# One crossbar DMA for the x of a tile, a later place for the second part of w_in, and a planner that dates the first weights later

## The chip, the cores and the metric

The kernel runs on one NeuronCore of a Trainium2 chip. The metric is the time of one execution on the device, in microseconds (us). Four executions of the kernel before gave 237.15, 240.17, 237.21 and 239.96 us, a median of 238.58 us. One further execution was recorded by the hardware profiler: it took 237.9 us, and the span between its first and its last instruction is 236.1 us.

The engines are called PE (TensorE, matrix products; its weight loads are listed apart as PEld), ACT (ScalarE), DVE (VectorE), POOL (GpSimd) and SP (SyncE, which issues most DMAs here). A DMA is issued by an engine's queue and moves its data by itself.

## What is computed

An attention in which some heads see all earlier positions and the others only a few first positions ("sinks") and a window, and behind it a dense layer with an unusual activation. The reference, cut to what matters:

```python
# q, k, v: [4 batches, 8 heads, 768 positions, 64]; n_sink 4, window 64
scores = q @ k.T / 8                     # per head
keep = causal if retrieval[head] else causal & (is_sink | in_window)
a = softmax(where(keep, scores, -1e9))
x = (a @ v) laid out as [3072 tokens, 512]
h = x @ w_in                             # [512, 2048]
g = h - tanh(h)
out = g @ w_out                          # [2048, 512], float32
```

## The kernel before, in words

**Tiling.** The 3072 tokens are cut into 12 tiles of 256 tokens (TT = 256), three to a batch (NG = 3), each of two blocks of 128 (NB = 2). Heads go in pairs: HP = 4 pairs, 128 columns each. For each tile and pair the kernel computes scores (`st_S`, matmul L971), their exponential on ACT (L991), masks on DVE, a product with v (`st_A`, matmul L1060, tile `av`), and the division by the row sum on DVE. What results is x of the tile, 256 tokens by 512 columns, in float16. The dense layer needs it transposed, as `xT`. With it `H_unit(t, u)` makes 256 of the 2048 hidden columns of tile t in 16 matmuls (L1165, tile `ph`, two accumulations of 4 column blocks each for two groups of 128 columns), tanh on ACT (L1178, `th`), and h - tanh(h) on DVE (L1185, `gt`). There are 8 units to a tile. `O_group` multiplies by w_out (L1224, tile `po`), ACT copies the result out (L1200) and SP stores it (L1212).

**How x is transposed.** Tiles 0 to 2 (the first batch) do it on PE: `st_X` transposes a pair's two blocks (L1138, tile `xp`) and ACT or DVE copies them from PSUM into `xT` (L853, L855). Tiles 3 to 11 are "ranked" (`ranked(t)`: heads sorted so that those that see everything come first). Their x is collected in one tile `x16t` of [128, 2 blocks, 8 heads, 64] by DVE (L1090), and `st_X_tile` turns it with crossbar DMAs that SP issues (L1118): one for each block of 128 tokens, 512 columns each, into `xT` of shape [128, 4, 256]. Each has its own key, and the matmuls of `H_unit` wait for both (`x_keys`). Crossbar DMAs of 1024 columns are in the kernel too: `cast_ranked` turns q and k of a block together (L727), two such DMAs for each ranked tile.

**Weights.** POOL issues the DMAs that load and cast weights: w_in in four parts of 512 columns (`load_w_in`, L415; the table `W_IN`), w_out in four parts (`load_w_out`, L429). Part j of w_in feeds units 2j and 2j+1 of a tile. The same POOL queue carries v of tile 1, q, k and v of tile 2 (`load_cast`, L392). All of these are chained by `behind`: each may be issued only after the one before it has been issued. So the order on the queue is: w_in part 1, v of tile 1 (two DMAs), w_in parts 2, 3 and 4, w_out part 1, q and k of tile 2 (four), w_out part 2, v of tile 2 (two), w_out parts 3 and 4.

POOL has other work in the same microseconds: it casts q and k of tile 1 from float32 to float16 (L675; four casts: q and k of the first heads, then q and k of the second heads), and it scales v by the heads' flags (L839, tile `vf`, two for tile 0).

**What sets the order.** No engine's order is written out. Each step is recorded by `op(engine, ns, fn, r, w, dma=...)` with a duration in ns, the keys that it reads and writes, and for a DMA its number of packets. `Plan.run` then plays the whole program through: each engine takes, of its steps that are ready, the one recorded first, and two DMA rings (POOL's and SP's) share the DMA time. The order that comes out is the order in which the instructions are issued; the engines keep to it on the chip whatever really comes late. L152 is where the planner says when a DMA starts to move data after its issue: 1200 ns for POOL's, 1000 or 400 ns for SP's.

```python
rings["POOL" if e == "POOL" else "SP"].append(
    [i, t + ns + (1200 if e == "POOL" else 1000 if t < 6000 else 400), each, packets * each / 16]
```

The second half of the file holds a second program, for the case that too many heads see everything; it isn't run with these inputs.

Of the kernel before, what the change touches and what calls it, by code (L numbers as in the profile page):

```python
# [8 lines left out]
FP16 = mybir.dt.float16  # L9
# [7 lines left out]
class Plan:  # L17
# [42 lines left out]
    def run(self, fill=None, until=None):  # L60
        self.fill = fill
        n = len(self.ops)
        users = [[] for _ in range(n)]
        followers = [[] for _ in range(n)]
        left = [0] * n
        for i, o in enumerate(self.ops):
            left[i] = len(o[3]) + (o[7] is not None)
            for d in o[3]:
                users[d].append(i)
            if o[7] is not None:  # L70
                followers[o[7]].append(i)
        ready = [0.0] * n
        free = dict.fromkeys(self.ENGINES, 800.0)
        queue = {e: [] for e in self.ENGINES}
        rings = {"SP": [], "POOL": []}
        now = 0.0
        self.start = [0.0] * n
        self.done = [0.0] * n
        order = []

        self.port = 0.0

        def at(i):

            return max(ready[i], self.port) if self.ops[i][6] else ready[i]

        def enqueue(i):
            queue[self.ops[i][0]].append(i)

        def finish(i, done):  # L90
            self.done[i] = done
            e, ns = self.ops[i][:2]
            for u in users[i]:
                to = self.ops[u][0]
                if to == e and e == "PE":
                    at = self.start[i] + ns
                else:
                    at = done + (60 if to == "PE" else 40)
                ready[u] = max(ready[u], at)
                left[u] -= 1  # L100
                if not left[u]:
                    enqueue(u)

        for i in range(n):
            if not left[i]:
                enqueue(i)
        while len(order) < n:
            t, e = min(
                [(max(free[e], min(at(i) for i in q)), e) for e, q in queue.items() if q],
                default=(1e12, None),  # L110
            )

            live = [r for r in rings.values() if r and r[0][1] <= now]
            nxt = min([r[0][1] for r in rings.values() if r and r[0][1] > now], default=1e12)
            if live:
                pk = sum(r[0][2] for r in live)
                end, r = min((now + r[0][3] * pk / r[0][2], k) for k, r in enumerate(live))
                stop = min(end, nxt, t)
                for x in live:
                    x[0][3] -= (stop - now) * x[0][2] / pk  # L120
                now = stop
                if end <= min(nxt, t):
                    i = live[r].pop(0)[0]
                    finish(i, now + 1300)
                    continue
                if nxt < t:
                    continue
            elif nxt < t:
                now = nxt
                continue  # L130
            now = max(now, t)
            i = min(
                (i for i in queue[e] if at(i) <= t), key=lambda i: self.ops[i][5]
            )
            queue[e].remove(i)
            _, ns, _, _, dma, _, port, _ = self.ops[i]
            if e == "PE" and t < 5600:
                ns *= 2
            self.start[i] = t
            order.append(i)  # L140
            free[e] = t + max(ns - self.OVERLAP[e], 40)
            if port:
                self.port = free[e]
            for u in followers[i]:
                ready[u] = max(ready[u], free[e])
                left[u] -= 1
                if not left[u]:
                    enqueue(u)
            if dma:
                packets, each = dma  # L150
                rings["POOL" if e == "POOL" else "SP"].append(
                    [i, t + ns + (1200 if e == "POOL" else 1000 if t < 6000 else 400), each, packets * each / 16]  # L152
                )
            else:
                finish(i, t + ns + self.RESULT[e])
        self.end = max(self.done)
        free = self.FROM
        for i in order:
            if self.ops[i][0] == "PE":
                idle = self.start[i] - free  # L160
                if self.fill and idle > 200 and i != until and self.FROM < free:
                    self.fill(int(idle * 0.5 / 107), 256)
                free = max(free, self.start[i] + self.ops[i][1])
                if i == until:
                    self.fill = None
            self.ops[i][2]()
# [3 lines left out]
def kernel(  # L170
# [98 lines left out]
    def program(first):  # L269
# [581 lines left out]
        def copy(e, dst, src):  # L851
            if e == "ACT":
                nc.scalar.copy(out=dst, in_=src)  # L853
            else:
                nc.vector.tensor_copy(out=dst, in_=src)  # L855
# [255 lines left out]

        def st_X_tile(t):

            xTs[t] = lazy(xt_pool, [128, HP, TT], FP16, "xT", f"xT{t}")
            for i in range(NB):
                op(
                    "SP", 1250,
                    lambda i=i: nc.sync.dma_start_transpose(  # L1118
                        out=xTs[t]()[:, :, i * 128 : i * 128 + 128],
                        in_=x16s[t]()[:, i, :, :].rearrange("p h d -> p (h d)"),  # L1120
                    ),
                    r=[("x16t", t)], w=[("xT", t, "all", i)], dma=(512, 22.0),
                )

        def x_keys(t):
            if ranked(t):
                return [("xT", t, "all", i) for i in range(NB)]
            return [("xT", t, c) for c in range(HP)]

        def st_X(n, tag="m", eng="DVE"):  # L1130
            t, hp = divmod(n, HP)
            if hp == 0:
                xTs[t] = lazy(xt_pool, [128, HP, TT], FP16, "xT", f"xT{t}")
            xp, key = bank([128, NB, 128], FP16, tag, f"xp{n}")

            def mm():
                for i in range(NB):
                    nc.tensor.transpose(  # L1138
                        out=xp()[:, i, :], in_=x16s[-1 - n]()[:, i, :, :], identity=ident16[:]
                    )  # L1140

            first_x.append(op("PE", 112, mm, r=[("x16", n), "ident"], w=[key]))
            op(
                eng, {"ACT": 373, "DVE": 290}[eng],
                lambda: copy(eng, xTs[t]()[:, hp, :], xp()[:].rearrange("p i c -> p (i c)")),
                r=[key], w=[("xT", t, hp)],
            )

# [6 lines left out]
        def H_unit(t, u):  # L1155
            if u == 0:
                gts[t] = lazy(g_pool, [128, NFB, TT], FP16, "gt", f"gt{t}")
            ph, key = bank([128, FU, TT], FP32, "h", f"ph{t}_{u}")
            for j in range(FU):

                def mm(j=j):
                    fb = u * FU + j
                    w, c0 = w_in_t[fb // 4]
                    for cb in range(HP):
                        nc.tensor.matmul(  # L1165
                            out=ph()[:, j, :], lhsT=w()[:, cb, c0 + fb % 4 : c0 + 512 : 4],
                            rhs=xTs[t]()[:, cb, :], start=(cb == 0), stop=(cb == HP - 1),
                        )

                op(  # L1170
                    "PE", 4 * 109, mm,
                    r=[("win", u * FU // 4)] + x_keys(t), w=[key],
                )
            th = lazy(th_pool, [128, FU, TT], FP32, "th", f"th{t}_{u}")
            tk = ("th", t * NFU + u)
            op(
                "ACT", 597,
                lambda: nc.scalar.activation(  # L1178
                    out=th()[:], in_=ph()[:], func=AF.Tanh, scale=1.0 / XS
                ),  # L1180
                r=[key], w=[tk],
            )
            op(
                "DVE", 687,
                lambda: nc.vector.scalar_tensor_tensor(  # L1185
                    out=gts[t]()[:, u * FU : (u + 1) * FU, :], in0=th()[:], scalar=-XS,
                    in1=ph()[:], op0=ALU.mult, op1=ALU.add,
                ),
                r=[key, tk], w=[("gt", t, u)],
            )  # L1190
# [131 lines left out]
            st_A(n, 1)  # L1322
            st_X(n, "o", "ACT")
        if first:
            load_w_in(*W_IN[1], ())
            load_w_in(*W_IN[2], ())
            scale_v(0, "POOL")
            load_w_in(*W_IN[3], ())
# [149 lines left out]
```

The softmax here doesn't subtract the row's maximum and nothing guards it: scores larger than these inputs give would overflow.

## Time and profile before, and how to read them

| | |
|---|---|
| four executions | 237.15, 240.17, 237.21, 239.96 us; median 238.58 us |
| the profiled execution | 237.9 us, span 236.1 us, granted PE clock 0.996 |
| PE | 223.6 us busy (95%) |
| ACT, DVE, POOL | 143.3 us (61%), 138.9 us (59%), 90.0 us (38%) |
| matmuls of x with w_in, L1165 | 768, 273 ns each |
| matmuls with w_out, L1224 | 400, 371 ns each |
| crossbar DMAs of xT, L1118 | 18, median 3.1 us from issue to landing |
| crossbar DMAs of q and k, L727 | 18, median 3.9 us |
| DMAs of w_in, L415 | 4, 512 KB each, 8.8 to 11.3 us from issue to landing |
| DMAs of w_out, L429 | 4, 512 KB each, 9.9 to 12.9 us |

All moments are microseconds from the start of the span. A line of the timeline gives the start, the duration, the engine, the line of the kernel, the operation, output and input, and how many such instructions follow each other; in brackets stands how long the engine was idle before it and what ended that. "SPq" is the issue of a DMA, not its transfer. The duration of a matmul includes its latency: successive matmuls overlap, so the start of the next says how long one really occupies PE. The view by windows gives the busy time of each engine in stretches of the span.

### The profile page before, as it was taken

To read this page: it belongs to the slowest core of one execution; us is meant where nothing else is said; L and a number is where in the kernel's file an instruction comes from. 1 tells how busy PE (TensorE), PEld (TensorE's weight loads), DVE (VectorE), ACT (ScalarE), POOL (GpSimd) and SP (SyncE) were. 2 spreads that over 40 slices of the span, in tenths; PEclk is the share of its full clock that TensorE was granted. 3 is DMA by queue.
4 is the path that set the end of the run, shared out by engine and by line. 5 is a ranking of instruction groups with operands and counts; after the bars stand their busy time and mean duration, and the time that the engine had idled before them with its cause. 6 is when DMAs were issued, how large, how long until landed. Compare 5 with 4: busy or idle time off the path is not lost. (4 is left out here: it accounts for less than half of the span.)

```text
span 236.1 us, 5930 instructions
## 1 busy us (share of the span) xinstructions
PE 223.6 (95%) x2234; PEld 158.3 (67%) x2234; DVE 138.9 (59%) x343; ACT 143.3 (61%) x221; POOL 90.0 (38%) x218
## 2 busy tenths in 40 slices
PE   7869899999999999999999999999999999999990
PEld 2446687766775787677767767767677677777660
DVE  3657667852688468658675647567676555434300
ACT  3877749883676498547668458456856754444410
POOL 5798350197709086470632929254000000000000
PEclk9999999999999999999999999999999999999998
DMA  5999999999899999988978996999303101411030
GB/s 129 265 198 207 193 186 219 215 229 219 114 219 190 227 231 173 231 186 178 202 165 221 162 237 72 242 217 151 86 0 89 45 2 47 90 44 45 2 113 29
DMA packets 106083, 35.83 MB, mean 152 GB/s; under 512 B 96194, under 2 KB 102594, under 8 KB 106050
## 3 DMA queue, kind: packets, MB, share of 16 engines
q1 hardware_dynamic: 94754, 30.03, 63.0%
q0 software_dynamic: 11008, 5.24, 16.8%
q8 instruction: 18, 0.29, 0.5%
q10 hardware_dynamic: 288, 0.14, 0.2%
q14 instruction: 15, 0.12, 0.2%
HBM read 27.27 MB, written 6.29 MB: 142 GB/s over the span
## 5 line engine op out<-in xcount | busy, mean ns | idle before, releaser
L1165 PE MATMUL ph<-xT,win 128*128 128x256 f16 x768 | 100.7, 273 | 1.8 <-DMA win<-in_moe_w_in_dram 1.0
L1224 PE MATMUL po<-wout,gt 128*128 128x512 f16 (+1 forms) x400 | 97.4, 371 | 0.3 <-ACT ot L1200 0.3
L1185 DVE SCALAR_TENSOR_TENSOR gt<-th,ph 128x512 f16<-128x512 f32 x96 | 65.4, 685 | 50.4 <-ACT th L1178 50.0
L1178 ACT ACTIVATE th<-ph 128x512 f32<-128x512 f32 x96 | 57.6, 601 | 60.8 <-PE ph L1165 56.4
L1165 PEld LDWEIGHTS <-win 128*128 128x128 f16 x768 | 80.6, 114 | 14.6 <-issue 2.2
L991 ACT ACTIVATE pt<-sc 128x1024 f16<-128x1024 f32 (+1 forms) x78 | 68.6, 927 | 8.8 <-PE sc L971 8.5
L1224 PEld LDWEIGHTS <-gt 128*128 128x128 f16 x400 | 36.4, 98 | 25.5 <-issue 1.0
L709 POOL CAST t<-raw_rqk 128x256 f16 x72 | 29.2, 443 | 56.5 <-DMA raw_rqk<-in_k_dram 41.3
L1060 PEld LDWEIGHTS <-pt 128*128 128x128 f16 x552 | 25.0, 97 | 9.7 <-DVE pt L1021 0.7
L1060 PE MATMUL av<-v,pt 128*128 128x65 f16 x304 | 25.5, 193 | 0.2 <-DVE pt L1021 0.2
L704 POOL CAST v<-raw_rv 128x128 f16 x72 | 21.6, 331 | 3.8 <-DMA raw_rv<-in_v_dram 3.8
L971 PE MATMUL sc<-qk 64*128 64x128 f16 (+1 forms) x412 | 23.1, 236 | 0.0
L1090 DVE TENSOR_TENSOR x16t<-av,rinv 128x128 f32 x72 | 20.8, 289 | 2.0 <-DMA xT<-x16t 0.2
L1200 ACT ACTIVATE ot<-po 128x512 f32<-128x512 f32 (+1 forms) x24 | 14.2, 593 | 10.7 <-PE po L1224 10.6
L971 PEld LDWEIGHTS <-qk 64*128 64x128 f16 x412 | 13.6, 94 | 9.7 <-issue 6.9
L1060 PE MATMUL av<-vf,pt 128*128 128x65 f16 x248 | 19.6, 193 | 0.0
L1016 DVE TENSOR_TENSOR pt<-pt,mS 128x512 f16<-128x512 f16 x24 | 10.9, 493 | 7.7 <-ACT pt L991 7.7
L1080 DVE RECIPROCAL rinv<-av 128x4 f32<-128x4 f32 x48 | 8.5, 178 | 11.2 <-PE av L1060 11.1
L1026 DVE TENSOR_TENSOR pt<-pt,m 128x1024 f16<-128x1024 f16 x16 | 11.9, 742 | 4.4 <-ACT pt L991 4.4
L780 POOL TENSOR_TENSOR vf<-v,rflagr 128x260 f16<-128x260 f16 x12 | 7.6, 640 | 0.0
L872 PEld LDWEIGHTS <-t 128*128 128x128 f16 x48 | 3.2, 97 | 5.8 <-ACT t L673 2.3
L459 PE MATMUL warm<-ones 128*128 128x512 f16 (+1 forms) x14 | 5.2, 527 | 1.2 <-POOL ones L454 1.2
(98 smaller groups left out, 95.0 us busy)
## 6 DMA issues: line engine op xcount, KB each, us to landing
out_dram<-ot SPq DMA_DIRECT2D x23, 256.0 KB, 2.4
raw_rqk<-in_q_dram SPq DMA_DIRECT2D x22, 256.0 KB, 4.9
raw_rqk<-in_k_dram SPq DMA_DIRECT2D x22, 256.0 KB, 4.8
raw_rv<-in_v_dram SPq DMA_DIRECT2D x18, 256.0 KB, 4.9
win<-in_moe_w_in_dram POOLq DMA_DIRECT2D x4, 512.0 KB, 9.8
wout<-in_moe_w_out_dram POOLq DMA_DIRECT2D x4, 512.0 KB, 11.7
raw_rv<-in_v_dram SPq DMA_DIRECT2D x4, 128.0 KB, 4.7
v<-in_v_dram POOLq DMA_DIRECT2D x4, 128.0 KB, 9.6
```

What stands on the lines that cost most here:

```text
L704: nc.gpsimd.tensor_copy(out=v1s[b]()[:, lo : lo + NB, rank : rank + 1, 0:D], in_=raw_of("v", t)[:, :, at, :],)
L709: nc.gpsimd.tensor_copy(out=t16[t % 2][:, :, :, rank : rank + 1, :], in_=raws["rqk", t][0]()[:, :, :, at, :],)
L971: nc.tensor.matmul(out=sc()[:, hh, o : o + nb * 128].rearrange("p (i c) -> p i c", c=128), lhsT=ks.rearrange("p i c -> p (i c)")[p_, jb * ...
L991: lambda pt=pt, gi=gi, wid=wid, sc=sc: nc.scalar.activation(out=pt()[:, :, 512 * gi : 512 * gi + wid], in_=sc()[:, :, 0:wid], func=AF.Exp, ...
L1026: nc.vector.tensor_mul(out=pv, in0=pv, in1=m4[:, h0 : h0 + 2, 256:512].unsqueeze(2).to_broadcast([128, 2, 2, 256]),)
L1060: nc.tensor.matmul(out=av()[:, i, hh, :], lhsT=pt()[:, hh, co : co + 128], rhs=vv, start=(jb == first_jb), stop=(jb == qb),)
L1090: nc.vector.tensor_mul(out=x16s[t]()[:, :, at, :], in0=av()[:, :, hh : hh + 1, 0:D], in1=rinv()[:, :, hh : hh + 1].unsqueeze(3).to_broadca ...
L1165: nc.tensor.matmul(out=ph()[:, j, :], lhsT=w()[:, cb, c0 + fb % 4 : c0 + 512 : 4], rhs=xTs[t]()[:, cb, :], start=(cb == 0), stop=(cb == HP ...
L1178: lambda: nc.scalar.activation(out=th()[:], in_=ph()[:], func=AF.Tanh, scale=1.0 / XS),
L1185: lambda: nc.vector.scalar_tensor_tensor(out=gts[t]()[:, u * FU : (u + 1) * FU, :], in0=th()[:], scalar=-XS, in1=ph()[:], op0=ALU.mult, op ...
L1200: nc.scalar.activation(out=ot()[:, c0:c1], in_=po()[:, c0:c1], func=AF.Copy, scale=1.0 / XS)
L1224: nc.tensor.matmul(out=po()[:, c0:c1], lhsT=gts[t]()[:, f, ts * 128 : ts * 128 + 128], rhs=w_out_t[f // 4]()[:, f % 4, c0:c1], start=(f == ...
```

## The change

Three edits, and what the planner makes of them.

```diff
@@ Plan.run: when POOL's DMA starts to move
-    [i, t + ns + (1200 if e == "POOL" else 1000 if t < 6000 else 400), each, packets * each / 16]
+    [i, t + ns + (1900 if e == "POOL" and t < 12000 else 1200 if e == "POOL" else 1000 if t < 6000 else 400), each, packets * each / 16]
@@ st_X_tile
-    xTs[t] = lazy(xt_pool, [128, HP, TT], FP16, "xT", f"xT{t}")
-    for i in range(NB):
-        op(
-            "SP", 1250,
-            lambda i=i: nc.sync.dma_start_transpose(
-                out=xTs[t]()[:, :, i * 128 : i * 128 + 128],
-                in_=x16s[t]()[:, i, :, :].rearrange("p h d -> p (h d)"),
-            ),
-            r=[("x16t", t)], w=[("xT", t, "all", i)], dma=(512, 22.0),
-        )
+    xTs[t] = lazy(xt_pool, [128, NB, HP, 128], FP16, "xT", f"xT{t}")
+    op(
+        "SP", 1250,
+        lambda: nc.sync.dma_start_transpose(
+            out=xTs[t]()[:].rearrange("p i c k -> p (i c) k"),
+            in_=x16s[t]()[:].rearrange("p i h d -> p (i h d)"),
+        ),
+        r=[("x16t", t)], w=[("xT", t, "all")], dma=(1024, 22.0),
+    )
@@ x_keys
-                return [("xT", t, "all", i) for i in range(NB)]
+                return [("xT", t, "all")]
@@ st_X
-                lambda: copy(eng, xTs[t]()[:, hp, :], xp()[:].rearrange("p i c -> p (i c)")),
+                lambda: copy(eng, xTs[t]()[:, :, hp, :], xp()[:]),
@@ H_unit
-                            out=ph()[:, j, :], lhsT=w()[:, cb, c0 + fb % 4 : c0 + 512 : 4],
-                            rhs=xTs[t]()[:, cb, :], start=(cb == 0), stop=(cb == HP - 1),
+                            out=ph()[:, j, :].rearrange("p (i k) -> p i k", i=NB),
+                            lhsT=w()[:, cb, c0 + fb % 4 : c0 + 512 : 4],
+                            rhs=xTs[t]()[:, :, cb, :], start=(cb == 0), stop=(cb == HP - 1),
@@ program, after tile 0
-            load_w_in(*W_IN[1], ())
+            load_w_in(*W_IN[1], t16_keys("k", 1, 0))
```

- **xT.** The tile's two blocks go in one crossbar DMA of 1024 columns instead of two of 512. `xT` is now laid out by block first, [128, 2, 4, 128], so the moving operand of the 768 matmuls of `H_unit` is two runs of 128 columns, 512 columns apart, instead of one run of 256. The copies of tiles 0 to 2 write the same two runs.
- **w_in part 2** is given a key to wait for: the float16 k of the first heads of tile 1, which POOL's second cast of tile 1 writes. Parts 3 and 4 and everything else of that chain come behind it.
- **The planner** dates the start of POOL's DMAs that are issued before 12 us by 1900 ns after their issue instead of 1200.

The order that comes out is another one on every engine. On POOL, from the first cast of tile 1 on (q0, k0, q1, k1 are its four casts):

```
before: q0, w_in 2, w_in 3, k0, scale v, scale v, q1, w_in 4, w_out 1, k1, q of tile 2 ...
after:  q0, scale v, k0, scale v, q1, w_in 2, w_in 3, w_in 4, k1, w_out 1, q of tile 2 ...
```

On PE the mask matmuls of a tile-1 unit (L958, two of 512 columns) now stand ahead of the first unit of `H_unit` instead of behind one and a half units. Around the first product with w_out the order was: two `po` steps, the second halves of attention, unit 6, unit 7 (its first half), transposes of tile 2, the transposes of x of tile 1's last pair, the other half of unit 7, tile 1's unit 0. It is now: one `po` step, half of unit 6, attention, the other half, the whole of unit 7, the transposes, the second `po` step, tile 1's unit 0. On SP the two xT issues of tile 3 followed the store of an output block directly; the single one now comes behind the load of one k block of tile 5 as well.

More of the change, by code (lines that the diff above doesn't have):

```diff
@@ L1132, in st_X @@
             if hp == 0:
-                xTs[t] = lazy(xt_pool, [128, HP, TT], FP16, "xT", f"xT{t}")
+                xTs[t] = lazy(xt_pool, [128, NB, HP, 128], FP16, "xT", f"xT{t}")
             xp, key = bank([128, NB, 128], FP16, tag, f"xp{n}")
```

## The prediction

> **What bounds the kernel now.** I read the time slices of the page first, then the windows of 6 us for how much of each PE is busy, then the timeline at the places where it isn't.
>
> ```profile
> span 236.1 us, 5930 instructions
> ...
> PE   7869899999999999999999999999999999999990
> ```
> ```profile
> 12.00:18.00 6.00, 4.22 (x53) 3.04 (x54) 2.95 (x9) 4.48 (x8) 6.00 (x10) 1.00 1.54 197
> 18.00:24.00 6.00, 5.33 (x71) 3.51 (x70) 4.58 (x12) 4.75 (x8) 4.64 (x7) 1.00 1.25 207
> 24.00:30.00 6.00, 5.51 (x60) 4.08 (x60) 3.77 (x11) 4.56 (x9) 2.31 (x3) 1.00 1.65 188
> ...
> 78.00:84.00 6.00, 6.00 (x60) 4.92 (x61) 3.64 (x9) 3.32 (x6) 0.78 (x2) 1.00 1.11 229
> ```
>
> The first column after the comma is PE. It is idle 1.78, 0.67 and 0.49 us in the windows from 12 to 30, then 0.32 in 30:36, and 0.99 in all from 36 to 78. From 78 on every window up to 228 shows 6.00 of 6.00: PE is the bound, and what any queue saves there is worth nothing. So the change can move the end only through what PE waits for before 78 us. There the weights come in:
>
> ```profile
> 12.04 1.49 POOL L415 DMA_DIRECT2D win<-in_moe_w_in_dram  x2
> 13.52 0.63 POOL L675 CAST t<-raw_rqk 128x512 f16<-128x512 f32 x1
> ...
> 24.39 0.88 POOL L392 DMA_DIRECT2D v<-in_v_dram  x1 [1.76 <-DMA win<-in_moe_w_in_dram]
> 27.01 0.87 POOL L392 DMA_DIRECT2D v<-in_v_dram  x1 [1.73 <-DMA win<-in_moe_w_in_dram]
> 29.43 0.55 POOL L429 DMA_DIRECT2D wout<-in_moe_w_out_dram  x1 [1.55 <-DMA wout<-in_moe_w_out_dram]
> ```
> ```profile
> 16.81 1.50 PE L1165 MATMUL ph<-xT,win 128*128 128x256 f16 x12 [0.97 <-DMA win<-in_moe_w_in_dram]
> ...
> 21.70 1.03 PE L1165 MATMUL ph<-xT,win 128*128 128x256 f16 x8
> ...
> 29.30 1.03 PE L1224 MATMUL po<-wout,gt 128*128 128x512 f16 x4
> ```
>
> POOL's three waits end 2.62 and 2.42 us apart, each at the landing of one weight part of 512 KB (w_in 3, w_in 4, w_out 1 by the order of the queue). They were issued at 12.8, 16.65 and 17.45, far from evenly. So the queue drains at its own rate, about 2.5 us a part, and the moment of issue doesn't matter while it is full. One step back from 24.39 puts w_in 2 at about 21.8, beside unit 2 of tile 0, which PE starts at 21.70; w_out 1 lands at about 29.3, beside PE's first `po` at 29.30. PE follows the queue there.
>
> The last place is tile 3, the first whose x goes by crossbar:
>
> ```profile
> 72.12 2.53 SPq L1118 DMA_TRANSPOSE xT<-x16t  x2
> ...
> 74.71 1.47 SPq L342 DMA_DIRECT2D raw_rqk<-in_k_dram  x1
> ...
> 77.92 1.50 PE L1165 MATMUL ph<-xT,win 128*128 128x256 f16 x12 [0.34 <-DMA xT<-x16t]
> ```
>
> And the DMA view of 70 to 80 us, whose first line gives the busy tenths of the engines in slices of 0.25 us:
>
> ```profile
> DMA  9999999999999999989990000079969999999999
> ```
>
> The DMAs are full without a gap to 75.5; what SP issues there waits in the queue behind what it issued before.
>
> **The change part by part**, against the profiled execution (237.9 us, span 236.1); it lies 0.7 us under the median, and I carry the difference over to 238.58.
>
> *w_in behind the cast, and POOL's new order.* Two issues (1.49 us at 12.04) leave the place ahead of the cast of k0, one scaling of v (2.07 us for two, so 1.03) enters it: k0 starts at 13.07 instead of 13.52. Q1's cast comes at about 14.6 instead of 16.10. Then three issues of 0.78 us run from 15.2 to 17.5, so k1 starts 0.5 earlier (17.99 before), w_out 1 is issued 0.6 later and the q loads of tile 2 (18.54) where they were. PE's wait for k0's cast (0.64 us at 14.20) shrinks by 0.45. But PE then meets the first w_in part at 16.81 all the same, where it already idled 0.97. Kept is only what was moved ahead of that wait: the two mask matmuls (0.59 us with latency; the next work began 0.53 after them), so 0.5 us. W_in 2 is issued at 15.2 instead of 12.04, 3.1 us later, but ahead of it the queue holds w_in 1 until 16.8 and half a part more of v until about 18, so it is still full when part 2 arrives, and the chain keeps its order. Behind it stand parts 3, 4 and all of w_out, none due sooner. So PE would be at unit 2 at 21.2 and wait there for a part that lands at 21.2 to 21.8, and by the first `po` (29.30, w_out 1 landing at 29.2 to 29.4) at most 0.1 is left. **-0.1 us**, between -0.5 (w_out 1 there long before) and 0.
>
> *The order between 29 and 35 us.* Up to tile 1's first unit PE has the same work in both orders; it began at 33.03. Now all of unit 7 precedes the transposes, and so on ACT its tanh (0.60) precedes the copies of q and k (0.65 for two) and of xT (0.39), for which tile 1 waits. From 29.30: one `po` step 0.43, unit 6 0.87, attention 0.43, unit 7 0.87, which ends at 31.9; tanh to 32.7, copies to 33.35, xT to 33.65. Tile 1 starts about 0.6 late. Before, its second half unit then waited for DVE (34.36 to 34.41) and the scores began at 35.38 after half a unit (0.43) more than they do now, at about 35.2: behind by 0.25. **+0.4**, between +0.25 and +0.6.
>
> *The single crossbar DMA of tile 3.* SP now issues a k load (0.58 to 1.47 by two rows of that line) and then one transpose: it starts at 72.7 to 73.6 and not at 72.12. Three bounds for its landing. By the median of the 1024-column ones for q and k, 3.9 us after issue: 76.6 to 77.5. By the second half before, issued at 73.4 and landed just before 77.92 (4.5 us): 77.2 to 78.1. And, the queue being full, by what now stands ahead of it: 256 KB of k at about 220 GB/s, which that view shows, are 1.2 us, so 77.9 + 1.2 = 79.1. PE would come there at 77.58 (77.92 less the 0.34 waited), less 0.1, plus 0.4: 77.88. At 77.5 or sooner the 0.34 vanishes and the sum at this place is 0.0; at 79.1 it is +1.2. I take 78.9, near the last, since the DMAs show no gap ahead: **+1.0 in all up to here**, the -0.1 and +0.4 included. The q and k transposes of tile 5 behind it keep the same work ahead of them, and their reader (the scores at 81.77) comes 1.0 later: no new wait.
>
> Here the Trainium skill's page "DMA: Bandwidth & Descriptors", section "Anatomy of one DMA — SWDGE (gpsimd) path", would say otherwise: about 2.0 us fixed for each DMA plus bytes at 436 GB/s, so that one large DMA beats two small ones. By it (it is fitted on POOL's path, not SP's; an estimate) 256 KB land 2.6 us after issue, PE waits for nothing, and the sum is 0.0. The trace has 3.1 and 3.9 us as medians and 4.5 here.
>
> *The other eight tiles.* SP's queue gains about 1.25 us each. No wait for xT is seen after 78 us, PE is full: 0. The same cover hides the eight other landings; gone, each would cost up to that 1.2.
>
> *The two-run operand.* 768 matmuls, 273 ns each. The nearest rows with two runs: mask matmuls whose 512 columns are two runs, 379 ns, against 379 for `po` with one run of 512; scores of two runs of 128, 274 ns against 273. **0**, within 1 ns each way (0.8 us). Eight copies on ACT and four on DVE write two runs; rows of that kind are 388 against 372 ns and 287 against about 290: 0.1 us off the path.
>
> *The new order from 36 to 78.* 0.65 us of waits there besides the 0.34 may go or double: **0**, within 0.65.
>
> Sum: +1.0. Span 237.1, execution 238.9, against the median **239.6 us**.
>
> **The rivals.**
>
> 1. *The start is won after all* (faster). If weights land by issue and engine readiness, not by a full queue, the earlier casts pull all of 12 to 30 together: 1.78 + 0.67 + 0.49 = 2.94 us less, 235.6 us. For it: idle time is there, and POOL's casts end some PE waits. Against: the 0.97 at 16.81 is a DMA's, and the even landings.
> 2. *The later w_in 2 is seen* (slower). If a part lands a fixed time after its issue (8.8 to 11.3 us in the table of this trace; w_in 2 took about 9.5), it lands at 15.2 + 9.5 = 24.7: unit 2, due at 21.7, waits 3.0, and everything in the chain behind shifts too: 241.6 us. It decides for "slower" once w_in 2 lands after 24.1. Against: the 2.5 us steps.
> 3. *xT lands late in many tiles* (slower). At +1.2 in three of the nine tiles: +3.6, 242.2 us. Against: one wait of 0.34 in nine tiles now.
> 4. *The change does nothing that PE sees*: the new tile-3 landing is hidden (at 77.5, as by the 3.9 us row) and the sum is 0.0: 238.6 us. For it: that median. Against: the full DMAs.
>
> **How the numbers follow.** A measurement of this kernel can tell about 1% from no change, 2.4 us. My forecast and rival 4 both lie within it: 0.49 together (0.31 and 0.18), with 237.7 to 240.6 as their own range (0.0 at tile 3 less the operand's 0.8; +1.2 there and the operand's 0.8). Rival 1: 0.20. Rival 2: 0.15. Rival 3, or an operand slower by over 3 ns a matmul: 0.16. So faster 0.20, same 0.49, slower 0.31. Range 235.6 to 242.0: it takes in rivals 1 and 2.
>
> **What would show it.** Right: w_in 3 and 4 and w_out 1 still end POOL's waits near 24.4, 27.0 and 29.4; PE starts unit 0 at 16.8, unit 2 at 21.2 to 21.8, `po` at 29.3, tile 1 at about 33.6; tile 3 starts its unit 0 at 77.9 to 79.1; L1164 stays at 273 ns; no idle PE after 80. Wrong: unit 2 after 24 (rival 2), PE idle below 1.5 us in all from 12 to 30 (rival 1), waits for xT in later tiles (rival 3).

## The result, and the profile after

The changed kernel takes **237.24 us** (median of 52 executions, 236.53 to 239.40), the kernel before 237.83 us (78 executions, 237.08 to 240.84). The ratio is 0.9973, with a 95% interval of 0.9962 to 0.9984: 0.6 us faster. Forecast was 239.6 us. Ratios here leave out executions that the chip disturbed; medians take all.

The profiled execution of the changed kernel took 237.28 us with a span of 235.4, against 237.9 and 236.1 before. So the two profiles differ by what the medians differ by, and can be laid side by side.

The page of the changed kernel:

```profile
span 235.4 us, 5922 instructions
...
PE   7878899999999799999999999999999999999992
```

Its view by windows; the first number after the comma is PE:

```profile
12.00:18.00 6.00, 4.46 (x52) 2.74 (x52) 2.91 (x9) 4.36 (x7) 5.43 (x8) 1.00 1.47 184
18.00:24.00 6.00, 5.24 (x73) 3.78 (x71) 4.58 (x12) 4.40 (x8) 5.22 (x8) 1.00 1.21 194
24.00:30.00 6.00, 5.32 (x59) 3.99 (x59) 3.87 (x11) 4.74 (x9) 2.06 (x3) 1.00 1.47 196
72.00:78.00 6.00, 4.73 (x50) 2.59 (x49) 4.21 (x14) 2.90 (x5) 5.19 (x15) 1.00 1.25 208
78.00:84.00 6.00, 5.40 (x55) 4.46 (x55) 2.65 (x6) 2.50 (x4) 2.80 (x8) 1.00 1.03 223
```

From 12 to 30 us PE is idle 1.54, 0.76 and 0.68 us, 2.98 in all, where it was 2.94: nothing is won there. From 72 to 84 it is idle 1.87 us, where it was 0.62. From 84 to 228 it is full in both. So the body of this kernel, up to its last matmul, is not faster as a whole, and yet the kernel is.

The POOL queue, with the new order in the first lines and the three waits for weights in the last:

```profile
13.03 0.60 POOL L675 CAST t<-raw_rqk 128x512 f16<-128x512 f32 x1
...
15.77 2.31 POOL L415 DMA_DIRECT2D win<-in_moe_w_in_dram  x3
...
24.69 0.89 POOL L392 DMA_DIRECT2D v<-in_v_dram  x1 [1.47 <-DMA win<-in_moe_w_in_dram]
27.23 0.87 POOL L392 DMA_DIRECT2D v<-in_v_dram  x1 [1.65 <-DMA win<-in_moe_w_in_dram]
29.70 0.55 POOL L429 DMA_DIRECT2D wout<-in_moe_w_out_dram  x1 [1.60 <-DMA wout<-in_moe_w_out_dram]
```

The waits end at 24.69, 27.23 and 29.70 instead of 24.39, 27.01 and 29.43, still 2.5 us apart, although part 2 of w_in was issued 3.7 us later than before (15.77 against 12.04). What PE meets of that, and the first tile whose x comes by crossbar:

```profile
17.17 1.07 PE L1164 MATMUL ph<-xT,win 128*128 128x256 f16 x8 [0.45 <-DMA win<-in_moe_w_in_dram]
...
21.91 1.06 PE L1164 MATMUL ph<-xT,win 128*128 128x256 f16 x8 [0.57 <-DMA win<-in_moe_w_in_dram]
...
29.49 0.59 PE L1224 MATMUL po<-wout,gt 128*128 128x512 f16 x2
...
78.60 1.03 PE L1164 MATMUL ph<-xT,win 128*128 128x256 f16 x8 [1.59 <-DMA xT<-x16t]
```
```profile
72.69 0.43 SPq L342 DMA_DIRECT2D raw_rqk<-in_k_dram  x1
73.23 3.28 SPq L1117 DMA_TRANSPOSE xT<-x16t  x1
76.56 0.58 SPq L342 DMA_DIRECT2D raw_rqk<-in_k_dram  x1
```

The DMA view of 70 to 80 us, busy tenths in slices of 0.25 us:

```profile
DMA  9999999999999999999999999950059755999999
```

The DMAs are full to 76.5, where they were full to 75.25; in both kernels xT lands behind the gap that follows. PE comes to tile 3 at 77.01 (78.60 less the 1.59 waited), 0.57 sooner than before, and starts there 0.68 later, because xT is late. (The k load ahead of it is that of tile 6; the section on the change says tile 5.)

The end. The last work of the program is a copy of the output on DVE, a store, and then on SP a row of waits: eight for the DMAs' semaphores, twelve for others, and three DRAINs. The eight are the semaphores on which the DMAs of SP and ACT report their landing, in turn: by the records of the trace each of the 129 DMAs before takes the next one of the eight. Their order at the end is fixed. Before:

```profile
230.19 0.42 DVE L1204 TENSOR_SCALAR ot<-po 128x256 f32<-128x256 f32 x1 [6.55 <-PEq L1441]
230.65 0.33 SPq L1212 DMA_DIRECT2D out_dram<-ot  x1
```
```profile
L1441 SPq EVENT_SEMAPHORE  x8: 17/17/17, 233.3 to 233.8; - x8
```
```profile
L1473 SPq EVENT_SEMAPHORE  x14: 17/28/28, 233.9 to 236.0; - x14
...
L1473 SPq DRAIN  x3: 7/7/136, 235.1 to 235.5; - x3
```

After:

```profile
230.96 0.42 DVE L1204 TENSOR_SCALAR ot<-po 128x256 f32<-128x256 f32 x1 [6.55 <-PEq L1441]
```
```profile
L1441 SPq EVENT_SEMAPHORE  x8: 17/17/17, 232.3 to 233.8; - x8
```
```profile
L1473 SPq EVENT_SEMAPHORE  x14: 17/28/28, 233.8 to 235.4; - x14
...
L1473 SPq DRAIN  x3: 7/7/13, 234.6 to 234.9; - x3
```

In a line of these views stand the durations in ns (least, median, most) and then the first and the last start. Until the last copy the changed kernel is 0.77 us behind (230.96 against 230.19). From there to the end of the span it takes 4.48 us where the kernel before takes 5.87, 1.39 less; -1.39 + 0.77 is the -0.62 measured. The records of SP's single instructions split the 1.39:

| from the start of the last copy | before | after | difference |
|---|---|---|---|
| to the issue of the last store | 0.46 | 0.45 | 0 |
| from there to its landing | 2.65 | 2.35 | -0.30 |
| the semaphore waits that are still to come | 0.54 (seven) | 0 (none) | -0.54 |
| from the eighth wait to the end | 2.22 | 1.69 | -0.53 |

Before, the last store reports on semaphore 100, the first in that order: the first wait lasts until it lands, at 233.30, and the seven others follow one by one until 233.84. After, it reports on 109, the last: seven waits are over by 232.82, while the store is still under way, and the eighth ends everything. The 127 DMAs of SP and two of ACT before leave a remainder of one when divided by eight, the 118 and two after leave none. The change's nine fewer crossbar DMAs did that. The last row of the table is mainly the first DRAIN: it starts 0.41 us after the wait ahead of it instead of 0.07, and takes 136 ns instead of 13. The landing's 0.30 is no effect of the change: the kernel with one crossbar only, profiled twice, has 2.33 and 2.68 us there.

### The profile page after: what moved, and what is told of

It is laid out like the page before. It is cut to its first block, busy times and chain, and to the rows that moved or that the text cites. A ratio compares the mean times of both kernels' runs of the same rounds, so it can differ in the third digit from the quotient of the medians.

```text
span 235.4 us, 5922 instructions
## 1 busy us (share of the span) xinstructions
PE 223.4 (95%) x2234; PEld 158.3 (67%) x2234; DVE 138.7 (59%) x343; ACT 143.2 (61%) x221; POOL 89.5 (38%) x218
## 5 line engine op out<-in xcount | busy, mean ns | idle before, releaser
L1164 PE MATMUL ph<-xT,win 128*128 128x256 f16 x768 | 100.8, 273 | 3.0 <-DMA xT<-x16t 1.6
L1164 PEld LDWEIGHTS <-win 128*128 128x128 f16 x768 | 80.7, 114 | 16.4 <-issue 3.1
L709 POOL CAST t<-raw_rqk 128x256 f16 x72 | 28.1, 431 | 53.1 <-DMA raw_rqk<-in_k_dram 38.3
```

The costliest lines, as they stand in the source:

```text
L709: nc.gpsimd.tensor_copy(out=t16[t % 2][:, :, :, rank : rank + 1, :], in_=raws["rqk", t][0]()[:, :, :, at, :],)
L1164: nc.tensor.matmul(out=ph()[:, j, :].rearrange("p (i k) -> p i k", i=NB), lhsT=w()[:, cb, c0 + fb % 4 : c0 + 512 : 4], rhs=xTs[t]()[:, :, ...
```

## The experiments

**Theory 1**: the gain lies after the last matmul, in how the program ends, and the body is slower by what xT costs at tile 3. **Theory 2**: the gain comes from the start, and the shorter end is chance. **Theory 3**: the single crossbar DMA quickens the body. All runs in one table; "end" is from the start of the last copy to the end of the span, "after wait 8" from the eighth semaphore wait to there, and the moments are those of each kernel's profile. The numbers for *before* and *after* are those of the first comparison; the ratios are against executions of the kernel before that were measured beside each.

| kernel | median us | ratio, interval | PE at tile 3 | xT issued | unit 0 | last copy | end | after wait 8 |
|---|---|---|---|---|---|---|---|---|
| before | 237.83 | | 77.58 | 72.12 | 77.92 | 230.19 | 5.87 | 2.22 |
| after | 237.24 | 0.9973 (0.9962-0.9984) | 77.01 | 73.23 | 78.60 | 230.96 | 4.48 | 1.69 |
| before, 7 small DMAs | 236.75 | 0.9969 (0.9947-0.9990) | 77.34 | 72.33 | 77.58 | 229.86 | 4.71 | 1.68 |
| before, 8 small DMAs | 237.37 | 0.9972 (0.9951-0.9993) | 77.85 | 72.37 | 78.24 | 230.51 | 5.20 | 1.68 |
| after, 1 small DMA | 237.87 | 1.0026 (0.9993-1.0058) | 76.71 | 72.25 | 78.51 | 230.75 | 5.32 | 1.69 |
| after, 7 small DMAs | 237.70 | 1.0002 (0.9984-1.0020) | 76.66 | 72.30 | 78.46 | 230.83 | 5.05 | 2.20 |
| one crossbar only | 236.40 | 0.9947 (0.9922-0.9971) | | | | | 4.47 | 1.69 |
| the same again | 236.45 | 0.9914 (0.9879-0.9949) | 78.02 | 73.03 | 78.37 | 230.63 | 4.82 | 1.69 |
| one crossbar, 1 small DMA | 236.93 | 0.9957 (0.9926-0.9989) | 77.52 | 72.08 | 77.82 | 230.05 | 5.03 | 1.69 |
| two crossbars | 239.19 | 1.0060 (1.0040-1.0079) | 76.59 | 72.62 | 78.37 | 232.24 | 5.54 | 2.22 |
| later date only | 239.05 | 1.0053 (1.0021-1.0085) | 77.30 | 72.85 | 79.05 | 233.05 | 5.57 | 2.22 |
| later w_in only | 239.03 | 1.0035 (1.0007-1.0062) | 77.43 | 71.54 | 77.43 | 231.41 | 5.61 | 2.20 |
| after, k behind xT | 237.03 | 0.9963 (0.9938-0.9989) | 76.47 | 72.50 | 77.69 | 230.40 | 4.86 | 1.69 |
| after, q and k behind xT | 236.83 | 0.9921 (0.9886-0.9956) | 75.30 | 70.75 | 76.06 | 229.73 | 4.49 | 1.69 |

### The end of the program

**Seven small DMAs in the kernel before.**

```diff
+    spare = const.tile([1, 16], FP16, name="spare")
...
+                for x in range(7):
+                    nc.sync.dma_start(out=spare[:, x : x + 1], in_=ones[0:1, 0:1])
```

> The kernel before with seven more DMAs on SP, of one element each, issued in SP's idle time between 9.5 and 31.7 us; they copy into a tile that nothing reads, so the result is the same. They move the last store from the semaphore that the end of the program waits for first to the one it waits for last, as in the changed kernel. Theory 1 (the change's gain lies after the last matmul, in the order of those waits, and its body is slower): the last DVE copy of the output starts at 230.2 as before (230.0 to 230.4), the time from there to the end falls from 5.87 to 4.5 to 5.4 us, and the run takes 0.5 to 1.4 us less than before, 236.4 to 237.4. Theory 2 (the gain comes from the start of the program, and the shorter end of the one profile is chance): nothing changes, 5.9 us at the end and 237.8 us, 237.6 to 238.0. Theory 3 (the single crossbar DMA itself quickens the body): the same as theory 2.

Its end (the lines have moved down by three):

```profile
L1444 SPq EVENT_SEMAPHORE  x8: 17/17/17, 231.2 to 232.9; - x8
```
```profile
L1476 SPq EVENT_SEMAPHORE  x14: 17/28/28, 233.0 to 234.5; - x14
...
L1476 SPq DRAIN  x3: 7/7/13, 233.7 to 234.0; - x3
```

The waits now begin at 231.2 and not at the landing, the long DRAIN is gone, the end takes 4.71 us, and the kernel is 1.0 us faster by the medians (236.75 against 237.77 measured beside it), though it does more work and nothing else in it was touched. (Its last copy, at 229.86, is a little ahead of the 230.0 to 230.4 that was expected.) Theories 2 and 3 fall: the kernel before gains as much as the changed one (ratios of 0.9969 and 0.9973) without any part of the change.

**Eight of them** (`range(8)`), which brings the last store back to the semaphore waited for first.

> The kernel before with eight DMAs of one element instead of seven: the last store is back on the semaphore waited for first (result the same). If the semaphore makes the gain of the run with seven: the end takes 5.2 to 5.9 us again and the time is 237.3 to 238.2. If the small DMAs themselves quicken the body or the end in some other way: 236.75 like the run with seven, 236.5 to 237.0.

```profile
L1444 SPq EVENT_SEMAPHORE  x8: 17/17/17, 233.5 to 234.0; - x8
```
```profile
L1476 SPq EVENT_SEMAPHORE  x14: 17/28/28, 234.1 to 235.7; - x14
...
L1476 SPq DRAIN  x3: 7/7/13, 234.8 to 235.2; - x3
```

The waits again begin at the landing (233.5) and take 0.54 us more, and the median is 0.6 us above that with seven. But it is still 0.46 under before (237.37 against 237.83), because the long DRAIN has not come back: that is a second effect, beside the order of the semaphores. The ratios alone, 0.9969 with seven and 0.9972 with eight, each good to about 0.5 us, do not tell the two kernels apart; the medians and SP's rows do, and the next pair does so by its ratios too.

**One small DMA in the changed kernel** (`range(1)`).

> The changed kernel with one more DMA of one element on SP in its idle time before 32 us (result the same), which moves the last store to the semaphore waited for first, as in the kernel before. Theory 1: the last DVE copy starts at 231.0 as in the changed kernel (230.8 to 231.2), the time from there to the end grows from 4.49 to 5.0 to 5.9, and the run takes 237.7 to 238.7 us, so as much as the kernel before or up to 0.9 us more. Theories 2 and 3: as the changed kernel, 237.24 (237.0 to 237.5).

```profile
L1444 SPq EVENT_SEMAPHORE  x8: 17/17/17, 233.8 to 234.4; - x8
```
```profile
L1476 SPq DRAIN  x3: 7/7/13, 235.2 to 235.5; - x3
```

The body stays (last copy 230.75), the waits begin at the landing (233.8), the end grows by 0.84 (0.54 for the seven waits, 0.28 for a slower landing), and the whole gain is lost: 237.87 against 237.24, with ratios whose intervals lie apart. No long DRAIN here either. What brings that one?

**Seven small DMAs in the changed kernel** (`range(7)`). SP's compiled program has 342 instructions in the kernel before, 334 in the changed one, 342 in this one; the traces show 138 fewer in each, 204, 196 and 204.

> The changed kernel with seven DMAs of one element more on SP before 32 us (result the same). The last store then lies on the semaphore waited for next to last, so the order of the waits should cost only one of the seven steps, 0.07 us. But SP's program has as many instructions as that of the kernel before, 342, where the changed kernel has 334. If the late DRAIN (0.41 us of idle time and 0.12 us more of its own) comes at a fixed count of SP's instructions, it is back: a DRAIN of 130 ns or more, an end of 4.9 to 5.4 us where the changed kernel has 4.5, and 237.5 to 238.0 us. If it belongs to the semaphore that is waited for first, or to chance: DRAINs of 13 ns at most, an end of 4.4 to 4.9 us, and 237.2 to 237.4 us.

```profile
L1476 SPq EVENT_SEMAPHORE  x14: 17/28/28, 233.7 to 235.8; - x14
...
L1476 SPq DRAIN  x3: 7/7/136, 234.9 to 235.3; - x3
```

It is back: 136 ns, 0.40 us after the wait ahead of it, 2.20 us after wait 8, and 237.70 us. Over all runs, 342 instructions go with a DRAIN of 136 ns at this place (before, two crossbars, later date, this one); 334, 336, 350 and 351 with 13 ns. The kernel with the later w_in alone has 341, and there the pause stands one instruction further on, ahead of the second DRAIN (0.39 us after the first, and 130 ns). So in these five the pause stands at one and the same count, ahead of the 200th of SP's instructions in the trace. The programs of 334 and 336 end before their 200th. But the count alone is no rule: in the kernel before with seven and with eight small DMAs (350 and 351) the 200th is one of the semaphore waits, and it follows the one ahead after 0.06 us, without a pause. What SP does in the pause stays open. The DMA records give a hint: in each of the five a DMA of kind "instruction", 8 KB on queue 14, starts 0.6 to 0.9 us after the late DRAIN has begun; in the other nine none starts in the last microsecond of the span. A load of instructions would fit, but no run here tests it.

### The single crossbar DMA alone

The change's edit of `st_X_tile`, `x_keys`, `st_X` and `H_unit`, with w_in and the date of before.

> Only the single crossbar DMA per tile; w_in and the planner's date as before. Here the issue for tile 3 follows the store directly, with no k load ahead, and the last store lands on the semaphore waited for last. Theory 1: the start is as before (unit 0 at 16.8, po at 29.3), tile 3 starts unit 0 at 77.6 to 78.0 because no k load is ahead of it, the last DVE copy starts at 230.0 to 230.4, the end takes 4.5 to 5.4 us: 236.4 to 237.4 us, under the changed kernel by up to 0.8. Theory 2: no part of the start is there, so 237.8, like before. Theory 3: the last DVE copy starts 0.5 us or more earlier than the 230.19 of before, at 229.7 or sooner.

The median is 236.40, as theory 1 had it, 0.8 under the changed kernel. Its profile can't serve for moments, since the first twelve matmuls with w_in ran at a granted clock of 0.50 (2.69 us instead of 1.50) and all behind them is 1.4 late. So it was measured once more:

> The kernel with only the single crossbar DMA once more, since in its first profile the early matmuls ran at a lower clock, and so that it stands beside the others of this call. If the body is that of before: unit 0 of tile 0 at 16.5 to 17.2, tile 3 at 77.5 to 78.2, the last DVE copy at 229.8 to 230.5, the end 4.4 to 4.9 us, 236.2 to 236.7 us. If the single crossbar DMA quickens the body: the last DVE copy at 229.6 or sooner.

```profile
73.03 1.45 SPq L1117 DMA_TRANSPOSE xT<-x16t  x1
```
```profile
78.37 1.47 PE L1164 MATMUL ph<-xT,win 128*128 128x256 f16 x12 [0.35 <-DMA xT<-x16t]
```

The wait at tile 3 is that of before (0.34), with one DMA as with two. This execution (237.28 us) is slower than its median of 236.45; it waited 1.30 us for the first part of w_in where before waited 0.97, and unit 0 of tile 3 and the last copy came 0.2 and 0.1 later than expected.

And with one small DMA more, so that it can stand beside the kernel before with eight:

> Only the single crossbar DMA per tile, with one DMA of one element more, which moves the last store to the semaphore waited for first (result the same). Against the run without it: if the order of the semaphores is worth the 0.54 us that its rows show, 236.8 to 237.2 us with an end of 5.0 to 5.4 us; if it is not, 236.3 to 236.6. Against the kernel before with eight small DMAs (237.37 us, the same semaphore, no late DRAIN): what is left is the body, and if the single crossbar DMA by itself changes nothing that PE sees, the last DVE copy starts at 230.0 to 230.6 and the time is 237.2 to 237.5.

The semaphore is worth 0.5 us here too (236.93 against 236.45). With the semaphore and the DRAIN alike, the single DMA is 0.44 us under the two (236.93 against 237.37, not measured side by side); 0.3 is also what 236.40 and 236.45 lie under 236.75. Neither is clear of the scatter: the intervals of the ratios (0.9926 to 0.9989 and 0.9951 to 0.9993) overlap. The moments show no reason: from the first product with w_out to the last copy it is 200.8 us in both profiles with one DMA, and 200.7 and 201.0 in the two of before with small DMAs. That rest stays open.

### The later w_in and the later date

**Both of them, with the two crossbar DMAs of before.**

```diff
-    [i, t + ns + (1200 if e == "POOL" else 1000 if t < 6000 else 400), each, packets * each / 16]
+    [i, t + ns + (1900 if e == "POOL" and t < 12000 else 1200 if e == "POOL" else 1000 if t < 6000 else 400), each, packets * each / 16]
...
-            load_w_in(*W_IN[1], ())
+            load_w_in(*W_IN[1], t16_keys("k", 1, 0))
```

> The later w_in and the planner's later date, with the two crossbar DMAs of before. SP's order has the k load of tile 5 ahead of the two of tile 3, and the last store lies on the semaphore waited for first. Theory 1: tile 3 starts unit 0 at 78.4 to 79.4, the last DVE copy starts at 230.7 to 231.5, the end takes 5.9 us as before: 238.3 to 239.2 us, slower than before by 0.5 to 1.4. Theory 2: as the changed kernel, 237.2 (237.0 to 237.5). Theory 3: as before or slower by the start's changes alone, 237.8 to 238.3, with an end of 5.9.

It is slower than before, as theory 1 had it, by 1.4 us; its last copy (232.24) is later than the 230.7 to 231.5 of that theory. Its body holds two waits that no theory had, at 95 and 111 us, for q and k (in the line: us in all, times, longest):

```profile
PE sc L971 <- DMA qk<-t: 1.2, 2, 0.8
```

Ahead of the first, SP issues two xT, a store, two loads and two qk, the last two taking 5.81 us from 86.85 on. So in company with the new order a second crossbar DMA per tile does cost SP something that PE sees, 1.2 us. This, and 0.9 us of the same wait in the run with the date alone, are the only places where the traces show two DMAs costing PE time.

**The date alone**, and **w_in alone** (each one half of the diff above).

> Only the planner's later date; w_in and the two crossbar DMAs as before. From the first product with w_out on, PE has nearly the order of the changed kernel, and SP that of the run with two crossbars. If the order that the date brings is what saves 0.75 us between the first product with w_out and the arrival at tile 3: 47.4 to 47.7 us between them, where before has 48.2. If it is the later w_in: 48.0 or more. In either case tile 3 waits 1.5 to 1.9 us for xT behind the k load, the score wait of 0.8 us at 95 us comes again, and with the end on the semaphore waited for first the time is 238.6 to 239.5.

> Only the later w_in, with the old date and the two crossbar DMAs. If the date makes the shorter order, 48.0 us or more from the first product with w_out to the arrival at tile 3; if the later w_in does, 47.4 to 47.7. If the later w_in is hidden by the full queue, unit 0, unit 2 and the first product with w_out start within 0.5 us of before's 16.8, 21.7 and 29.3; if it is seen, unit 2 starts after 23. The k load is ahead of the crossbar DMAs and the last store on the semaphore waited for first: 238.3 to 239.5 us.

The date alone: the first product with w_out at 29.64, PE at tile 3 at 77.30, 47.66 us later; xT makes it wait 1.75 there, and the scores wait 0.9 in all for q and k. With w_in alone it is 48.22 (29.21 to 77.43), as before (48.28). So the date makes the order that is shorter, by 0.6. (For w_in alone the comparison is weaker: PE's order around tile 3 is another one there, and tile 3 waits for nothing.) With w_in alone the starts are 16.90, 21.64 and 29.21 against 16.81, 21.70 and 29.30: a part issued later behind a full queue isn't seen. Each alone is slower than before by 1.2 us. With w_in alone no wait tells why: in that order PE is busy 224.4 us instead of 223.6, and idle 0.3 more from 12 to 228.

### Why xT is late at tile 3

**The k load taken from ahead of it**, in the changed kernel:

```diff
+                        if first and fast and (nm, t) == ("k", 2 * NG):
+                            P.ops[at][3].add(turned[NG])
```

> The changed kernel, with both loads of k of tile 6 kept until the crossbar DMA of tile 3's xT has been issued, so that the xT issue follows the store again. The last store stays on the semaphore waited for last. Theory 1 (the k load ahead costs the body its 1.25 us at tile 3, and the end is a matter of the semaphores): tile 3's wait for xT falls from 1.6 to 0 to 0.5 us, the last DVE copy starts at 229.3 to 230.0 instead of 230.96, the end stays at 4.4 to 4.7 us, and the run takes 235.7 to 236.4 us. Rival (xT is late because the single DMA itself is slow, whatever lies ahead): the wait stays at 1.2 us or more and the time at 237.0 to 237.5.

```profile
72.50 1.30 SPq L1120 DMA_TRANSPOSE xT<-x16t  x1
```
```profile
77.69 1.47 PE L1167 MATMUL ph<-xT,win 128*128 128x256 f16 x12 [1.22 <-DMA xT<-x16t]
```

The rival has it: the wait is 1.22 and the time 237.03. The issue comes 0.73 sooner than in the changed kernel and xT 0.91 sooner, but PE comes 0.54 sooner too (76.47).

**The two loads of q as well** (`nm in "qk" and t == 2 * NG`).

> The changed kernel, with both loads of q of tile 6 as well as those of k kept until the crossbar DMA of tile 3's xT has been issued. If xT is late because four issues of q and k keep SP and the DMAs busy ahead of it (2.4 us of SP for the two of q alone), it now lands before PE comes: no wait for xT at tile 3, or under 0.3 us, the last DVE copy starts at 229.0 to 229.8, the end takes 4.4 to 4.9 us, and the run takes 235.5 to 236.4 us, under every kernel so far. If something else holds xT back (its data, or a crossbar DMA that takes 4 us and more by itself), the wait stays at 0.8 us or more and the time at 236.7 to 237.2.

```profile
70.75 1.25 SPq L1120 DMA_TRANSPOSE xT<-x16t  x1
```
```profile
76.06 0.60 PE L1167 MATMUL ph<-xT,win 128*128 128x256 f16 x4 [0.76 <-DMA xT<-x16t]
```

The wait lies between the two cases that were expected (under 0.3, or 0.8 and more), but the rival's point holds: with four loads taken from ahead of it, 1 MB, xT is still used 5.31 us after the start of its issue. SP had issued nothing for 1.7 us before it, and the DMAs of this run, busy tenths from 70 to 80 us, run dry before xT moves:

```profile
DMA  9999999499970599900003999999999996249999
```

From 74.25 to 75.25 they are all but idle; xT lands at 76.02. So no full queue holds it there.

In the other kernels with one DMA, it is 5.37 (after), 6.26, 6.16, 5.19, 5.34 and 5.74 us; with two, 5.25 to 6.20 where PE waited for them. So at tile 3 xT comes 5.2 to 6.3 us after the start of its issue: with one DMA 5.4 to 6.3 behind a k load and 5.2 to 5.7 without one, and it moves when the issue moves. My theory that the k load delays it by its 1.2 us in the DMA queue falls; what the load does is to take its place in SP's order, and to lengthen the issue of a single DMA behind it (3.28 us instead of 1.25 to 1.45), which may add half a microsecond. Why it takes 5 us is open. This version has the earliest last copy of all (229.73), but its executions scatter (235.42 to 239.60; the ten that the ratio takes have a median of 236.17), and against the kernel with one crossbar only its ratio says nothing (0.9921 and 0.9914, measured side by side).

## Why the prediction was wrong

The direction was wrong: +1.0 us was forecast, -0.6 came. Most of it is one step.

1. **The time after the last matmul: the step that failed.** The sum had no term for it. "PE is the bound" was read from windows that end at 228, and the 5.9 us from the last copy on were carried over as if nothing in the change touched them. The change removes nine DMAs from SP, and that moved the last store to another semaphore (-0.54) and took a pause out of SP's last instructions (-0.53); a quicker landing by chance made it -1.39 in these profiles. Over all fourteen profiles the landing takes 2.33 to 2.72 us, with no relation to the kernel. A look at the order in which SP waits at the end, and a count of DMAs modulo eight, would have given the -0.54; the pause could not have been priced from the trace of before alone.

2. **W_in behind the cast: right.** -0.1 was forecast. Unit 0, unit 2 and the first product with w_out start at 17.17, 21.91 and 29.49 in the changed kernel, 0.2 to 0.4 later than before, but at 16.87, 21.63 and 29.20 in the one with a small DMA more, which is the same up to there but for that. Runs differ by as much at the start by themselves: with before's order the first product with w_out starts anywhere from 29.19 to 29.82 (the profile with the low clock aside). Rivals 1 and 2 are refuted: PE's idle time from 12 to 30 is 2.98 us, not under 1.5, and unit 2 is not after 24.

3. **The order from 29 to 35: the sign was wrong.** +0.4 was forecast. From the first product with w_out to the scores of tile 1 it takes 5.61 us (29.49 to 35.10), where it took 6.08 (29.30 to 35.38): -0.47. My count made the whole of tile 1's unit 0 wait for the last copy into xT:

```profile
32.90 0.49 PE L1164 MATMUL ph<-xT,win 128*128 128x256 f16 x3
33.80 0.27 PE L1164 MATMUL ph<-xT,win 128*128 128x256 f16 x1 [0.41 <-ACT xT L853]
```

   Only the fourth matmul needs the last pair. Three start at 32.90, not at 33.65, and the fourth waits 0.41. (The count also slips by 0.09: 33.35 and 0.39 are 33.74.) With what is won later (0.3 between 36 and 77, priced at nothing, within 0.65), the order gives -0.76 up to tile 3 (47.52 us from the first product with w_out, against 48.28).

4. **The single crossbar DMA at tile 3: right in size, for another reason.** Unit 0 was put at 78.9, and started at 78.60; the last copy is 0.77 late where +1.0 was the sum. But the bound I took, the k load's 256 KB ahead in a full queue, is not what holds xT: taking it away moves xT only about as far as it moves the issue. The DMA line shown for that bound speaks against it: the DMAs are full to 75.25, not 75.5, and then all but idle to 76.5, while the two xT of before land at 77.27 and 77.87, behind that gap. PE came at 77.01 and not at 77.88, so the wait is 1.59 where the sum had 1.0; because PE waits for xT there in any case, what the order had won is lost again, and the body hangs on the landing. That the landing was put within 0.3 us on a wrong ground is luck. Nearer was the row of before itself, 5.80 us from the start of the first issue to use (77.92 less 72.12). With the issue at 73.23 that would have given 79.0, without any queue.

   The Trainium skill's page "DMA: Bandwidth & Descriptors", section "Anatomy of one DMA — SWDGE (gpsimd) path", gave an estimate of 2.6 us here. The trace has 2.7, 4.2 and 5.3 us as least, median and most of the nine. The measurement decides: its saving of a fixed cost per DMA was not what counted.

5. **The two-run operand: right.** L1164 has 273 ns a matmul, as L1165 had. **The other eight tiles: right.** No wait for xT is seen after tile 3, and PE is full from 84 on. So rival 3 is refuted, and so is rival 4, as the landing was not hidden.

Together: order -0.76, longer wait at tile 3 +1.25, start +0.19, the rest +0.09, which is the +0.77 of the body; the end -1.39. By medians the end is worth about -1.1 (before with seven small DMAs against before, 1.0; its two lasting terms, 1.07), so that the body of the changed kernel is about 0.5 us slower than that of before. The change's one useful part is the crossbar edit: with it alone the kernel takes 236.4 us, 0.8 less than with all three, and no version tried is measurably faster. Of the 1.4 us that it gains over before, 1.0 is what seven small DMAs alone bring.

## What to carry to other kernels

When PE is full to the end, the time behind its last matmul is the part that a change elsewhere can still move: count what ends the program as well, and above all which of its last waits the last store answers. Before a gain of a few tenths of a microsecond is put down to the work that was changed, add a few idle DMAs to the old kernel and see whether they give the same. And an operation that lands late isn't necessarily queued behind what stands before it: move its neighbours away, and see whether it moves by more than its own issue does.

## What the runs showed of the hardware

- Eight semaphores, used in turn by the DMAs of SP and ACT, are waited for one after the other at the end, 0.07 to 0.10 us each once they are due. A last store on the first one costs 0.54 us against one on the last.
- In the five kernels whose SP program has 341 or 342 instructions, SP takes 0.39 to 0.41 us instead of 0.07 to the 200th that the trace shows; it is a closing DRAIN, and takes 130 or 136 ns instead of 7 or 13. The programs of 334 and 336 end before their 200th; those of 350 and 351 show no such pause there. The Trainium skill's page "VectorE: DVE Perf Modes", section "The DRAIN you can't avoid", calls the DRAINs around a program constant, about 12 ns. In nine of the fourteen profiles SP's three at the end agree with that (7 to 13 ns), and in the five with 341 or 342 instructions one of the three does not.
- Tile 3's xT is used 5.2 to 6.3 us after the start of its issue, and the issue of a single one of 1024 columns takes SP 1.25 to 1.45 us, or 3.3 to 4.0 us directly behind a load of k. In the version with q and k behind it the DMAs are all but idle from 74.25 to 75.25, and it lands at 76.02.
